# Sliding-window attention, start of the kernel: two of the first four row blocks of x turned by a transposing DMA, and one V chain moved ahead of the last Q and K group

## The chip, the cores and the metric

One core of one Trainium2 chip. The metric is device time of a whole execution in microseconds (us); medians of several runs are quoted. A ratio is the mean time of one kernel's fast runs over that of the other's fast runs of the same rounds, with a 95% interval, so it is not quite the ratio of two medians.

## The reference

Two independent problems A and B, outputs put side by side. Each is (x is 2048 x 1024, bf16):

```python
qkv = (x @ wqkv).reshape(B, S, 3, H, Dh).transpose(2, 0, 3, 1, 4)   # H = 32 heads of Dh = 32
scores = einsum("bhqd,bhkd->bhqk", q, k) * Dh ** -0.5
mask = (i - j >= 0) & (i - j < 256)                                  # sliding window
o = einsum("bhqk,bhkd->bhqd", softmax(where(mask, scores, -1e9)), v)
out = o.transpose(0, 2, 1, 3).reshape(B, S, D) @ wo
```

## The kernel before

TensorE does projections (Q, K, V, output), scores and attention sums. All of it is one static program: 180 steps. A step is the scores of four 128 x 128 blocks for four heads, one exponential over them on ScalarE, and then as many projection matmuls as a build-time clock finds room for ("filler"):

```python
def session(now):                      # the head of a step
    st = ps_st.tile([P, 4, SLOTS, P], F32, name="st")     # one buffer of four PSUM banks
    ...                                # scores on TensorE into st
    nc.scalar.activation(out=pt..., in_=st..., func=ACT.Exp, ...)

def new_pp():                          # a projection chain takes one of two PSUM banks
    clock.chain()
    return ps_proj.tile([P, 512], F32, name="pp")

def evacuate(out, in_, engines=("act", "dve")):           # ... and is copied out of it
    if clock.evacuate(engines) == "act":                  # which engine: by the build-time clock
        nc.scalar.copy(out=out, in_=in_)
    else:
        nc.vector.tensor_copy(out=out, in_=in_)

def emit(now, budget):                 # filler: matmuls of the chains, by deadline
    done = 0.0
    while (current or chains) and done < budget - ...:
        ...
```

The order in which chains come and the engine that copies each are fixed at build time. PSUM's eight banks: four for scores (`st`), two for attention sums (`acc`), two for projections (`pp`).

The start: x is loaded row-wise and turned on TensorE, block by block of 128 rows, for the first four blocks; all later rows come by transposing DMA.

```python
load_wqk(0, 0, nc.scalar)
for a in range(QB):                                        # QB = 4 row blocks
    nc.sync.dma_start(out=xrow[a], in_=problems[0][0][a * P:(a + 1) * P, :])
    if a == 1:
        load_wqk(0, 1, nc.sync)
load_wv(0, 0, CT, nc.sync)
new_x(0, 1)
load_x(0, 1)                                               # transposing DMA, rows 512 to 1023
...
warm = ps_proj.tile([P, 512], F32, name="pp")
keep_warm(6)                                               # dummy matmuls
...
flip(0)              # 8 transposes on TensorE, copied out half by ScalarE, half by VectorE
keep_warm(4)
flip(1)
keep_warm(3)
first(0, 0)          # Q of rows 0..255
flip(2)
flip(3)
first(1, 0)          # K of rows 0..255
first(0, 256)        # Q of rows 256..511, then its copy
first(1, 256)        # K of rows 256..511, then its copy
emit(0, chains[0].size)      # one V chain (rows 0..255); then the steps begin
```

Of the kernel before, what the change touches and what calls it, by code (L numbers as in the profile page):

```python
# [9 lines left out]
F32 = mybir.dt.float32  # L10
# [8 lines left out]
P = 128  # L19
# [7 lines left out]
QB = 4  # L27
SLOTS = 4
# [50 lines left out]
def _fast_path(ctx, tc, cfg, problems, outs, consts, certify):  # L79
    nc = tc.nc  # L80
# [8 lines left out]
    clock = _Clock()  # L89
# [27 lines left out]
    ps_st = ctx.enter_context(tc.tile_pool(name="ps_st", bufs=1, space=PSUM))  # L117
    ps_acc = ctx.enter_context(tc.tile_pool(name="ps_acc", bufs=2, space=PSUM))
    ps_proj = ctx.enter_context(tc.tile_pool(name="ps_proj", bufs=2, space=PSUM))
# [6 lines left out]
    blank = top[:].bitcast(BF16)  # L126

    def new_x(pi, k):
        xT[(pi, k)] = xpool.tile([P, CT, 512], BF16, name="xT")

    def load_x(pi, k, a=0, n=QB, c0=0, c1=CT):
        lo, hi = a * P, (a + n) * P
        nc.sync.dma_start_transpose(
            out=xT[(pi, k)][:, c0:c1, lo:hi],
            in_=problems[pi][0][k * 512 + lo:k * 512 + hi, c0 * P:c1 * P])

    def wsrc(pi):
        return problems[pi][1].rearrange("(ct p) (k n) -> p ct k n", p=P, k=3)
# [4 lines left out]
    def load_wqk(g, which, queue, lo=0, hi=CT):  # L143
        pi, t = divmod(g, T)
        queue.dma_start(out=wqk[g][:, lo:hi, which, :],
                        in_=wsrc(pi)[:, lo:hi, which, t * P:(t + 1) * P])

    def new_wv(m):
        wv[m] = wvp.tile([P, CT, VG * P], BF16, name="wv")

    def load_wv(m, lo, hi, queue):
        pi, mm = divmod(m, T // VG)
        w_ = VG * P
        queue.dma_start(out=wv[m][:, lo:hi, :],
                        in_=wsrc(pi)[:, lo:hi, 2, mm * w_:(mm + 1) * w_])
# [9 lines left out]
    def qk_tiles(g):  # L165
        if g not in qks:
            qks[g] = (qkp.tile([P, S], BF16, name="qT"), qkp.tile([P, S], BF16, name="kT"))
        return qks[g]

    def by_columns(out, lo, hi, lhsT, rhs, start, stop):  # L170
        if whole[0]:
            nc.tensor.matmul(out[:, lo:hi], lhsT=lhsT, rhs=rhs, start=start, stop=stop,  # L172
                             skip_group_check=True)
            return
        for c in range(0, P, 32):
            nc.tensor.matmul(out[c:c + 32, lo:hi], lhsT=lhsT[:, c:c + 32], rhs=rhs, start=start,  # L176
                             stop=stop, tile_position=(0, c), skip_group_check=True)
# [4 lines left out]
    def add_or(dst):  # L182
        def f():
            nc.vector.tensor_tensor(out=top[:], in0=top[:], in1=dst.bitcast(I32),
                                    op=ALU.bitwise_or)
        side.append((COST["or"], f, False))

    def evacuate(out, in_, engines=("act", "dve")):
        if clock.evacuate(engines) == "act":
# [4 lines that stand above are left out]
    def new_pp():  # L194
        clock.chain()
        return ps_proj.tile([P, 512], F32, name="pp")

    def qk_steps(g, which, k, lo=0, hi=512, st_=None, last=True):
        pi = g // T
        st_ = {} if st_ is None else st_  # L200
        steps = []
        for ct in range(CT):
            def f(ct=ct):
                if "pp" not in st_:
                    st_["pp"] = new_pp()
                by_columns(st_["pp"], lo, hi, wqk[g][:, ct, which, :], xT[(pi, k)][:, ct, lo:hi],
                           ct == 0, ct == CT - 1)
                clock.pe += NS_MM * (hi - lo) / 512.0
                if ct == CT - 1 and last:
                    dst = qk_tiles(g)[which][:, k * 512:(k + 1) * 512]  # L210
                    evacuate(dst, st_["pp"][:])
                    add_or(dst)
            steps.append((NS_MM * (hi - lo) / 512.0, f))
        return steps
# [138 lines left out]
    chains = []  # L353
# [39 lines left out]
    def start_chain(now):  # L393
        for n, c in enumerate(chains):
            if c.early <= now:
                current.extend(chains.pop(n).steps)
                return True
        return False

    def run_side():  # L400
        cost, f, last = side.pop(0)
        f()
        clock.dve = max(clock.dve, clock.pe) + cost
        if last:
            clock.norms.append(clock.dve)

    def emit(now, budget):
        done = 0.0
        while (current or chains) and done < budget - 0.5 * (current[0][0] if current else NS_MM):
            if not current and not start_chain(now):  # L410
                break
            ns, f = current.pop(0)
            f()
            done += ns
            if side and (clock.dve < clock.pe + 100.0 or len(side) > 8):
                run_side()
# [124 lines left out]
    rows = opool.tile([P, T, 512], BF16, name="oT")  # L541
    new_x(0, 0)
    new_wqk(0)
    new_wv(0)
    xrow = [rows[:, 2 * a:2 * a + 2, :].rearrange("p t n -> p (t n)") for a in range(QB)]
    load_wqk(0, 0, nc.scalar)
    for a in range(QB):
        nc.sync.dma_start(out=xrow[a], in_=problems[0][0][a * P:(a + 1) * P, :])
        if a == 1:
            load_wqk(0, 1, nc.sync)  # L550
    load_wv(0, 0, CT, nc.sync)
    new_x(0, 1)
    load_x(0, 1)
    new_wqk(1)
# [6 lines left out]
            new_wv(1)  # L561
            load_wv(1, 0, CT, nc.sync)

    warm = ps_proj.tile([P, 512], F32, name="pp")

    def keep_warm(n):
        for _ in range(n):
            nc.tensor.matmul(warm[:], lhsT=blank[:, 0:P], rhs=blank[:, 0:512], start=True, stop=True)  # L568

    keep_warm(6)  # L570
    flips = [ps_acc.tile([P, 512], F32, name="acc") for _ in range(2)]
    flips = [f[:] for f in flips]
    flips.append(ps_st.tile([P, 4, SLOTS, P], F32, name="st")[:, 0].rearrange("p a q -> p (a q)"))
    flips.append(None)
    held = [{}, {}]

    def flip(a):
        if a == 3:
            flips[a] = ps_acc.tile([P, 512], F32, name="acc")[:]
        f = flips[a].bitcast(BF16).rearrange("p (ct q) -> p ct q", q=P)  # L580
        for ct in range(CT):
            nc.tensor.transpose(out=f[:, ct, :], in_=xrow[a][:, ct * P:(ct + 1) * P],  # L582
                                identity=ident[:])
        dst = xT[(0, 0)][:, :, a * P:(a + 1) * P]
        half = CT // 2
        nc.scalar.copy(out=dst[:, :half, :], in_=f[:, :half, :])
        nc.vector.tensor_copy(out=dst[:, half:, :], in_=f[:, half:, :])

    def first(which, lo):
        for _, f in qk_steps(0, which, 0, lo, lo + 256, held[which], last=lo > 0):  # L590
            f()

    flip(0)
    keep_warm(4)
    flip(1)
    keep_warm(3)
    first(0, 0)
    flip(2)
    flip(3)
    first(1, 0)  # L600
    first(0, 256)
    first(1, 256)
    emit(0, chains[0].size)

    sealed = first_use(G - 1, NQ - 1, 0)
    for now in range(END):
# [3 lines left out]
        while due and due[0][0] <= now:  # L610
            _, pg, pk = due.pop(0)
# [14 lines left out]
    while due:  # L626
        _, pg, pk = due.pop(0)
# [132 lines left out]
def kernel(  # L760
# [48 lines left out]
    with tc.manual_schedule():  # L809
        with ExitStack() as fctx:  # L810
            _fast_path(fctx, tc, cfg, problems, outs, consts, [reduce_bits, decide])
# [40 lines left out]
```

## Time and profile before

| | before |
|---|---|
| median (6 runs) | 609.76 us |
| TensorE busy | 593.6 us, 98% of the span |
| first useful projection | 7.56 us |
| first scores | 13.83 us |
| waits of TensorE for ScalarE's copies | 4, together 1.6 us |

The prediction shows the lines of these. Two things help to read them. In a timeline line the columns are start, time, engine, line of the program, operation, operands, count, and in brackets the idle time ahead of it with what ended it. And the records have holes: of 330 matmuls of Q and K on 512 columns that this program has in its undivided form, the trace of before holds 291. The 3.5 us that TensorE seems to wait for "issue" are such holes (fewer matmul records than weight loads, 12786 against 12838 here), and busy times of two kernels are not comparable to a per cent. Starts are.

### The profile page before, as it was taken

What the parts mean: (1) busy time and instruction counts of PE and PEld (TensorE: products, weight loads), DVE (VectorE), ACT (ScalarE), POOL (GpSimd) and SP (SyncE); (2) the same over time, 40 slices, a digit from 0 to 9 for tenths busy, and PEclk for the clock granted to TensorE, in tenths of its full rate; (3) what the DMA queues carried; (4) which work ended last, traced back from release to release, by engine and by line L of the source; (5) the groups of instructions that cost most, each with busy time, mean ns of one, the idle gap of its engine ahead of it and who ended that gap; (6) DMA issues with size and microseconds to landing.
All of it is one profiled execution on the core that took longest, in us unless ns stands there. A gap on an engine that the chain in (4) does not pass through costs nothing.

```text
span 607.6 us, 28768 instructions
## 1 busy us (share of the span) xinstructions
PE 593.6 (98%) x12786; PEld 344.3 (57%) x12838; DVE 468.4 (77%) x1199; ACT 441.1 (73%) x376; POOL 326.3 (54%) x630
## 2 busy tenths in 40 slices
PE   8999999999999999999999999999999999999996
PEld 6555466656655756564556756655455665545443
DVE  1677889898898898897888887898888887897200
ACT  3778887788888887877778877777776777785332
POOL 0565666665666666556555565555555655554000
PEclk9999999999999999999999999999999999999999
DMA  9833110111015501442111100112021040113222
GB/s 234 182 92 89 37 38 3 38 38 39 3 38 90 114 14 30 82 101 77 38 37 38 38 4 8 33 37 81 2 68 34 4 106 21 55 58 120 72 79 64
DMA packets 86802, 35.47 MB, mean 58 GB/s; under 512 B 65552, under 2 KB 86160, under 8 KB 86672
## 3 DMA queue, kind: packets, MB, share of 16 engines
q1 hardware_dynamic: 85632, 33.31, 22.2%
q8 instruction: 102, 1.67, 1.2%
q10 hardware_dynamic: 1040, 0.26, 0.2%
q14 instruction: 28, 0.23, 0.1%
HBM read 17.83 MB, written 8.39 MB: 43 GB/s over the span
## 4 chain that ended last, share of the span: by engine, by line
PE 96%; ACT 2%; issue 1%; DMA 1%; ACTq 0%
PE pp L176 44%; PE pp L172 28%; PE acc L513 13%; PE st L451 10%; ACT pt L459 1%; DMA oT<-in_A_x_dram 1%; PE acc L582 0%; PE pp L568 0%; ACT kT L190 0%; ACT vt L190 0%; PE st L582 0%; ACT osb L190 0%; PE pp L805 0%; ACTq L190 0%
## 5 line engine op out<-in xcount | busy, mean ns | idle before, releaser
L459 ACT ACTIVATE pt<-st 128x2048 bf16<-128x2048 f32 x180 | 338.0, 1878 | 91.6 <-PE st L451 73.5
L471 POOL TENSOR_SCALAR_AFFINE_SELECT pt<-pt 128x512 bf16<-128x512 bf16 x224 | 154.5, 690 | 145.7 <-ACT pt L459 143.1
L467 POOL TENSOR_SCALAR_AFFINE_SELECT pt<-pt 128x512 bf16<-128x512 bf16 x256 | 179.2, 701 | 85.8 <-ACT pt L459 85.8
L524 DVE RECIPROCAL rinv<-acc 128x128 f32<-128x128 f32 x128 | 122.0, 953 | 57.0 <-PE acc L513 56.4
L176 PE MATMUL pp<-xT,wqk 128*32 128x512 bf16 x2712 | 163.1, 379 | 0.0
L481 DVE TENSOR_TENSOR both<-pt 128x512 bf16<-128x512 bf16 x224 | 137.1, 651 | 0.0
L176 PEld LDWEIGHTS <-wqk 128*32 128x32 bf16 x2712 | 69.3, 97 | 54.2 <-issue 0.4
L172 PE MATMUL pp<-xT,wqk 128*128 128x512 bf16 (+1 forms) x323 | 76.7, 369 | 4.1 <-issue 2.4
L176 PE MATMUL pp<-wv,xT 128*32 128x256 bf16 x2436 | 75.9, 273 | 0.0
L451 PE MATMUL st<-qT,kT 32*128 32x384 bf16 (+2 forms) x1488 | 71.5, 269 | 0.1
L176 PEld LDWEIGHTS <-xT 128*32 128x32 bf16 x2436 | 63.8, 97 | 6.2
L529 DVE STREAM_SHUFFLE wide<-rinv 128x128 f32<-128x128 f32 x256 | 64.6, 298 | 0.0
L513 PE MATMUL acc<-pt,vt 128*32 128x128 bf16 (+1 forms) x2160 | 63.3, 239 | 0.0
L172 PE MATMUL pp<-wo_sb,oT 128*128 128x512 bf16 (+1 forms) x269 | 59.3, 373 | 1.3 <-issue 0.9
L451 PEld LDWEIGHTS <-kT 32*128 32x128 bf16 x1488 | 22.2, 92 | 64.5 <-issue 63.3
L190 ACT CAST osb<-pp 128x512 bf16<-128x512 f32 (+1 forms) x52 | 30.0, 577 | 39.1 <-PE pp L172 24.4
L531 DVE TENSOR_TENSOR oT<-acc,wide 128x256 bf16<-128x256 f32 x128 | 54.3, 425 | 4.4
L176 PE MATMUL pp<-wo_sb,oT 128*32 128x512 bf16 x952 | 55.6, 379 | 0.0
L172 PEld LDWEIGHTS <-wqk 128*128 128x128 bf16 x362 | 33.4, 98 | 37.0 <-issue 6.8
L172 PE MATMUL pp<-wv,xT 128*128 128x256 bf16 x415 | 50.9, 273 | 1.4 <-ACT kT L190 0.6
L513 PEld LDWEIGHTS <-vt 128*32 128x32 bf16 x2160 | 35.9, 96 | 26.4 <-issue 24.1
L172 PEld LDWEIGHTS <-xT 128*128 128x128 bf16 x415 | 38.9, 98 | 12.0 <-issue 6.1
(46 smaller groups left out, 386.5 us busy)
## 6 DMA issues: line engine op xcount, KB each, us to landing
out_dram<-osb SPq DMA_DIRECT2D x63, 128.0 KB, 1.8
wqk<-in_B_wqkv_dram SPq DMA_DIRECT2D x32, 128.0 KB, 2.5
wqk<-in_A_wqkv_dram SPq DMA_DIRECT2D x24, 128.0 KB, 2.7
wo_sb<-in_A_wo_dram SPq DMA_DIRECT2D x16, 128.0 KB, 2.2
wv<-in_B_wqkv_dram SPq DMA_DIRECT2D x16, 128.0 KB, 2.8
wo_sb<-in_B_wo_dram SPq DMA_DIRECT2D x16, 128.0 KB, 2.4
oT<-in_A_x_dram SPq DMA_DIRECT2D x4, 256.0 KB, 5.4
wv<-in_A_wqkv_dram SPq DMA_DIRECT2D x2, 512.0 KB, 5.9
```

The source lines that it names most:

```text
L172: nc.tensor.matmul(out[:, lo:hi], lhsT=lhsT, rhs=rhs, start=start, stop=stop, skip_group_check=True)
L176: nc.tensor.matmul(out[c:c + 32, lo:hi], lhsT=lhsT[:, c:c + 32], rhs=rhs, start=start, stop=stop, tile_position=(0, c), skip_group_check=True)
L190: nc.scalar.copy(out=out, in_=in_)
L451: nc.tensor.matmul(st[:, r, a:b, :], lhsT=kT[32 * r:32 * r + 32, j * P:(j + 1) * P], rhs=qT[32 * r:32 * r + 32, q * P:(q + b - a) * P], st ...
L459: nc.scalar.activation(out=pt[:, :, :n, :].rearrange("p r a q -> p r (a q)"), in_=st[:, :, :n, :].rearrange("p r a q -> p r (a q)"), func= ...
L467: nc.gpsimd.affine_select(out=blk, in_=blk, pattern=[[0, 4], [1, P]], compare_op=ALU.is_ge, fill=0.0, base=0, channel_multiplier=-1)
L471: nc.gpsimd.affine_select(out=blk, in_=blk, pattern=[[0, 4], [-1, P]], compare_op=ALU.is_gt, fill=0.0, base=0, channel_multiplier=1)
L481: nc.vector.tensor_tensor(out=both[:, :, h, :], in0=pts[s0][:, :, a0, :], in1=pts[s1][:, :, a1, :], op=ALU.add)
L513: nc.tensor.matmul(acc[32 * r:32 * r + 32, o:o + w_], lhsT=lhsT, rhs=src[:, r, :, :], start=(x == 0), stop=(x == len(moves) - 1), tile_pos ...
L524: nc.vector.reciprocal(out=rinv[:], in_=acc[:, 2 * P:3 * P])
L529: nc.vector.stream_shuffle(out=wide[:, h * P:(h + 1) * P], in_=rinv[:], mask=[16 * h] * 32)
L531: nc.vector.tensor_tensor(out=oTs[(pi, k)][:, t, (p % 2) * 256:(p % 2 + 1) * 256], in0=acc[:, 0:256], in1=wide[:], op=ALU.mult)
```

## The change

The intent, as I read it: save 16 of the 32 transposes on TensorE by letting the DMA turn blocks 2 and 3, begin useful work earlier by treating blocks 0 and 1 one at a time, and fill the time until the DMA's rows arrive with the first V chain. The dummies and the first Q and K move into the score banks, which are not in use yet.

```diff
-    for a in range(QB):
+    for a in range(2):
         nc.sync.dma_start(out=xrow[a], in_=problems[0][0][a * P:(a + 1) * P, :])
-        if a == 1:
+        if a == 0:
             load_wqk(0, 1, nc.sync)
     load_wv(0, 0, CT, nc.sync)
+    load_x(0, 0, 2, 2)
     new_x(0, 1)
     load_x(0, 1)
 ... (cut)
-    warm = ps_proj.tile([P, 512], F32, name="pp")
+    spare = ps_st.tile([P, 4, SLOTS, P], F32, name="st")[:].rearrange("p r a q -> p r (a q)")
+    warm = spare[:, 1]
 ... (cut)
-    held = [{}, {}]
+    held = [{"pp": spare[:, 2]}, {"pp": spare[:, 3]}]
 ... (cut)
-    def first(which, lo):
-        for _, f in qk_steps(0, which, 0, lo, lo + 256, held[which], last=lo > 0):
-            f()
+    def first(lo, hi):
+        for which in range(2):
+            for _, f in qk_steps(0, which, 0, lo, hi, held[which], last=hi == 512):
+                f()

     flip(0)
-    keep_warm(4)
+    keep_warm(3)
+    first(0, P)
     flip(1)
     keep_warm(3)
-    first(0, 0)
-    flip(2)
-    flip(3)
-    first(1, 0)
-    first(0, 256)
-    first(1, 256)
+    first(P, 2 * P)
+    emit(0, chains[0].size)
+    first(2 * P, 4 * P)
+    clock.banks = [clock.pe, clock.pe]
     emit(0, chains[0].size)
```

So two V chains now stand ahead of the first scores, not one.

More of the change, by code (lines that the diff above doesn't have):

```diff
@@ L544, in _fast_path @@
     new_wv(0)
-    xrow = [rows[:, 2 * a:2 * a + 2, :].rearrange("p t n -> p (t n)") for a in range(QB)]
+    xrow = [rows[:, 2 * a:2 * a + 2, :].rearrange("p t n -> p (t n)") for a in range(2)]
     load_wqk(0, 0, nc.scalar)
-    for a in range(QB):
+    for a in range(2):
         nc.sync.dma_start(out=xrow[a], in_=problems[0][0][a * P:(a + 1) * P, :])
-        if a == 1:
+        if a == 0:
             load_wqk(0, 1, nc.sync)
     load_wv(0, 0, CT, nc.sync)
+    load_x(0, 0, 2, 2)
     new_x(0, 1)
@@ L562, in _fast_path @@
             load_wv(1, 0, CT, nc.sync)
-    warm = ps_proj.tile([P, 512], F32, name="pp")
+    spare = ps_st.tile([P, 4, SLOTS, P], F32, name="st")[:].rearrange("p r a q -> p r (a q)")
+    warm = spare[:, 1]
     def keep_warm(n):
         for _ in range(n):
-            nc.tensor.matmul(warm[:], lhsT=blank[:, 0:P], rhs=blank[:, 0:512], start=True, stop=True)
+            nc.tensor.matmul(warm, lhsT=blank[:, 0:P], rhs=blank[:, 0:512], start=True, stop=True)
     keep_warm(6)
-    flips = [ps_acc.tile([P, 512], F32, name="acc") for _ in range(2)]
-    flips = [f[:] for f in flips]
-    flips.append(ps_st.tile([P, 4, SLOTS, P], F32, name="st")[:, 0].rearrange("p a q -> p (a q)"))
-    flips.append(None)
-    held = [{}, {}]
+    flips = [ps_acc.tile([P, 512], F32, name="acc")[:] for _ in range(2)]
+    held = [{"pp": spare[:, 2]}, {"pp": spare[:, 3]}]
     def flip(a):
-        if a == 3:
-            flips[a] = ps_acc.tile([P, 512], F32, name="acc")[:]
         f = flips[a].bitcast(BF16).rearrange("p (ct q) -> p ct q", q=P)
```

## The prediction

> **What bounds the kernel now.** I read the page first (busy times, then the chain that ended last), then TensorE's waits, then the first 17 us of the chain, then single waits further on.
>
> From the page of the kernel before, busy time and chain:
>
> ```profile
> PE 593.6 (98%) x12786; PEld 344.3 (57%) x12838; DVE 468.4 (77%) x1199; ACT 441.1 (73%) x376; POOL 326.3 (54%) x630
> ...
> PE 96%; ACT 2%; issue 1%; DMA 1%; ACTq 0%
> ```
>
> TensorE is busy for 98% of the span and makes up 96% of the chain. So the end moves only by what is taken from or given to TensorE: fewer columns streamed, or fewer stalls. Everything else is hidden unless it stalls TensorE.
>
> The waits of TensorE over the whole span:
>
> ```profile
> PE pp L172 <- ACT vt L190: 1.0, 2, 0.5
> PE pp L172 <- ACT kT L190: 0.6, 2, 0.4
> PE pp L172 <- DVE oT L531: 0.3, 2, 0.2
> ```
>
> The columns are total us, times, longest. Only four waits for ScalarE come up in 600 us, 1.6 us together. I return to them, as a reordered program can have more.
>
> The head of the chain, 0 to 17 us (start, us, what):
>
> ```profile
> 0.80 3.50 DMA oT<-in_A_x_dram
> ...
> 4.34 1.04 PE acc L582 x8
> 5.38 0.90 PE pp L568 x4
> 6.28 0.60 PE acc L582 x8
> 6.89 0.65 PE pp L568 x3
> ...
> 7.56 1.06 PE pp L172 x8
> 8.62 0.45 PE st L582 x8
> 9.06 0.45 PE acc L582 x8
> 9.51 4.39 PE pp L172 x40
> 13.90 0.33 PE st L451 x8
> 14.23 2.07 PE pp L172 x17
> ```
>
> L582 is a transpose of a row block of x, L568 a dummy matmul that keeps the clock up, L172 a projection, L451 the first scores. The reader sees that useful projection starts only at 7.56 us, after two blocks are turned and copied, and that 0.90 us then go to turning two more blocks.
>
> The copies between a transpose and its first use, from the timeline (start, us, engine):
>
> ```profile
> 5.42 0.59 ACT L586 COPY xT<-acc 128x512 bf16<-128x512 bf16 x1 [2.84 <-PE acc L582]
> 6.04 0.42 DVE L587 COPY xT<-acc 128x512 bf16<-128x512 bf16 x1 [4.73 <-ACT xT L586]
> ...
> 6.92 0.59 ACT L586 COPY xT<-acc 128x512 bf16<-128x512 bf16 x1 [0.92 <-PE acc L582]
> ```
>
> The DVE half starts after the ACT half has ended (6.01), so a block is usable in halves. Block 1: transposes at 6.26, first matmul at 7.56, 1.30 us later.
>
> SyncE's issues from the timeline:
>
> ```profile
> 3.29 0.43 SPq L154 DMA_DIRECT2D wv<-in_A_wqkv_dram  x1
> 3.77 8.07 SPq L133 DMA_TRANSPOSE xT<-in_A_x_dram  x1
> ```
>
> The second 512 rows of x come by a transposing DMA, issued at 3.77 and landing 10.2 us later (the view of its tile), at about 14.0.
>
> **What the Trainium skill says.** (1) "TensorE: Matmul & The Clock Gate", section "Wait — 56ns, not 53.3ns?": warm matmuls follow each other at columns / 2.4 GHz plus about 2.5 ns, 55.6 ns for 128 columns. The trace agrees: 8 transposes in 0.45 us are 56 ns each, and 40 matmuls of 256 columns in 4.39 us are 110 ns each. So the row's "mean ns" (273 for 256 columns) is latency, not cost. (2) "PSUM — Partial Sum Buffer", section "PSUM bank collisions raise a hardware error": two engines must not touch one bank and quadrant at once, ScalarE against VectorE too. The trace shows the consequence above: VectorE's half of a copy out of the same bank waits for ScalarE's. The new code keeps that. (3) "Advanced Engine Details and Errata", section "X-Bar Transpose (TRN2)": transposing DMAs are as fast as plain ones. Here roughly: in windows of half a microsecond the stretch of only transposing traffic (10.5 to 13 us) moves 290 GB/s, the plain stretch before (6.3 to 9 us) 325.
>
> **The change part by part.** The order of the two programs, compared engine by engine, gives the counts.
>
> TensorE's work. Removed: 16 transposes and one dummy of 512 columns. Added: nothing in columns, but Q and K of the first 256 rows come in 32 matmuls of 128 columns in place of 16 of 256; that costs 32 x 56 - 16 x 110 = 30 ns. Moved: 16 V matmuls (4096 columns) from after the first scores to before them. All else has the same columns, and the count of switches between full, row-tiled and column-tiled matmuls is the same. Gross saving 0.90 + 0.22 us of TensorE's instructions.
>
> What it means for the clock time of the head, stepped with the durations above:
> - Block 0 turned at 4.34, ScalarE's half ready at 6.05, VectorE's at 6.50. Q, K on 128 columns: 4 matmuls at 6.05, the other 12 from 6.50 at 56 ns, to 7.17.
> - Block 1 turned at 7.17. Ready 1.30 us later, 8.47 (first half) and 8.92 (second). Here TensorE has only three dummies to do: a stall of about 0.85 us that the old order did not have after 7.56. Q, K of block 1 to 8.92 + 12 x 0.056 = 9.6.
> - V of blocks 0, 1: 16 x 0.110 = 1.76, to 11.35. Q, K of blocks 2, 3: 16 x 0.110 = 1.76, to 13.1. V of blocks 2, 3: to 14.9. First scores with their switch, 0.42: 15.3.
>
> The old kernel had done the same work (first scores and both V chains) at 15.92, where the timeline starts the next Q chain. So the head gains about 0.6 us, not the 1.1 of the removed instructions: turning block 1 now sits between useful pieces with its copy exposed. The scores start 1.1 us later than before (14.95 against 13.83), but 4096 columns (1.71 us) are already done; the following steps carry less filler until that is paid back, and TensorE stays the bound.
>
> The rest of the program. The scheduler's estimate is fixed at build time, so later steps get another mix of filler. A step (there are 180) is the scores of four blocks, one exponential on ScalarE, and projections as filler. Projections have two PSUM banks. If one step ends two chains' worth so that a third chain starts in it, the third needs the bank of the first; when ScalarE empties that bank it does so behind the step's exponential. One such case in the chain, with step 44's:
>
> ```profile
> 141.00 0.02 issue
> 141.03 1.88 ACT pt L459
> 142.90 0.49 ACT vt L190
> 143.39 0.04 issue
> 143.43 0.38 PE pp L172
> ```
>
> I went through the order of both programs for steps in which a third chain starts early while its bank is emptied by ScalarE in that step. For each, the start of the third chain after the first score matmul is 0.46 us (scores and switch), plus 0.62 us if attention sums are in the step, plus columns / 2400 per us. Before: steps 20, 44, 73, 79, at 2.59, 2.27, 2.38, 2.27 us. These are exactly the four waits in the trace (at 72, 141, 224 and 242 us); the view gives 0.5, 0.5 for the V ones at 2.27, and 0.4 and 0.2 for the others. So the wait is about 2.8 us minus that start. (Steps 129 to 159 have starts of 2.9 and later and show no wait, which fits.) After: steps 17, 23, 28, 41, 73, 79, at 2.38, 2.27, 2.59, 2.49, 2.38, 2.27: 0.4 + 0.5 + 0.2 + 0.3 + 0.4 + 0.5 = 2.3 us. That is 0.7 us more than the 1.6 of before. Cases emptied by VectorE (no exponential ahead) show no wait in the trace and number 11 before, 10 after.
>
> Sum: 609.6 - 0.6 + 0.7 = 609.7; nearly nothing. As the extra waits are certain in order but the head could gain a little more (a landing earlier with less traffic), I say 609.6 us.
>
> **Rivals.** (a) The full gain: the head saves 1.1 us or more and the extra waits vanish in other slack. For it: 98% busy, so each saved column counts. Against: four waits of this kind are on the chain already, one for one with the order. It would give 608.3. (b) The transposing DMA becomes the wait. Blocks 2 and 3 (0.5 MB) follow V's weights; by then 1.57 MB are queued ahead, against 1.09 MB moved by 6.3 us and 325 GB/s after, so weights end at about 7.9 and, at 290 GB/s, the blocks at 9.7, landing near 10.3. Needed at 11.35. The next 512 rows land near 14, as before, because the bytes ahead are the same; needed at 15.3 instead of 15.9. For this rival: margins of only 1 us, and issue of 512 rows took 5.6 to 8.1 us of SyncE, so a slow issue could add 1 to 2 us: 610.5 to 611.5. Against: the issue of 8.07 us was held up by the traffic ahead, as the later two took 6.00 and 5.61. (c) ScalarE becomes the bound in the early steps, since scores start later and less filler covers each exponential. A step needs 0.45 + 1.88 us for scores and exponential, TensorE's steps are about 2.9 us apart: slack of half a microsecond. If it did, all of the head's gain is lost, 610.3.
>
> **Range and chances.** Head 0.6 with an error of about 0.5, waits 0.7 with about 0.4, between runs the old kernel spreads by 1.2 us in all (609.18 to 610.35). So 608.5 to 610.7 eight times in ten. Two per cent are 12 us, more than the whole head could give or a late transfer take: faster 0.01, within 2% 0.98, slower 0.01.
>
> **What would show it.** Right: useful projection from about 6.05 us; scores at about 15; the chain after the head again TensorE; the waits of TensorE for ScalarE's copies up from four to six, about 2.3 us, near steps 17, 23, 28 and 41; TensorE's matmul count down by about 58 as some V columns run whole. Wrong: a wait of TensorE for a DMA of x in the head (rival b); waits for the exponential's PSUM in the first steps (c); a head that ends later than 15.9; or four or fewer ScalarE waits with a time below 608.5.

## The result, and the profile after

| | before | after |
|---|---|---|
| median (6 runs each) | 609.76 us (609.18 to 610.35) | 611.19 us (610.68 to 611.58) |
| ratio | | 1.0022 (1.0009 to 1.0035) |
| span of the profiled run | 607.6 us | 608.9 us |
| first useful projection | 7.56 us | 6.04 us |
| first scores | 13.83 us | 15.71 us |
| scores and both V chains done | 15.92 us | 16.04 us |

Within 2%, as said, but 1.4 us slower where I had said nearly nothing, and outside my range of 608.5 to 610.7.

The waits of TensorE over the span, after (total us, times, longest):

```profile
PE pp L172 <- ACT vt L190: 1.3, 3, 0.5
PE st L172 <- ACT qT L190: 0.7, 1, 0.7
PE pp L172 <- ACT kT L190: 0.6, 2, 0.4
PE pp L172 <- ACT qT L190: 0.4, 1, 0.4
```

The three rows with `pp` are the six stalls I had counted from the order: 1.3 + 0.6 + 0.4 = 2.3 us, as predicted. The row with `st` is new: Q and K of the start lie in `st`. It is in the head. The timeline there, after:

```profile
9.46 1.91 PE L172 MATMUL pp<-wv,xT 128*128 128x256 bf16 x16
...
11.29 1.03 PE L172 MATMUL st<-xT,wqk 128*128 128x256 bf16 x8
...
12.36 0.58 ACT L190 CAST qT<-st 128x512 bf16<-128x512 f32 x1 [0.37 <-PE st L172]
...
12.99 1.03 PE L172 MATMUL st<-xT,wqk 128*128 128x256 bf16 x8 [0.67 <-ACT qT L190]
...
15.71 0.40 PE L451 MATMUL st<-qT,kT 32*128 32x384 bf16 x8
```

The V chain and Q start within 0.2 us of my steps (9.6 and 11.35). Then K's eight matmuls stand still for 0.67 us until ScalarE has copied Q out, though they write another bank. The scores come at 15.71, where I had 14.95. The built program has this wait in it, at K's first matmul of the last group; the same matmul of the kernel before has none:

```
after   L172 Matmult st<-xT,wqk 128x256 [waits Activation_49]
before  L172 Matmult pp<-xT,wqk 128x256
```

The head is done (scores and both V chains) when the next Q chain starts. Before, in the line that the prediction speaks of, and after:

```profile
15.92 0.81 PE L172 MATMUL pp<-xT,wqk 128*128 128x512 bf16 x2
```

```profile
16.04 1.25 PE L172 MATMUL pp<-xT,wqk 128*128 128x512 bf16 x5
```

The stalls further on, seen in one step, number 17. In before (scores, next scores):

```profile
63.08 0.40 PE L451 MATMUL st<-qT,kT 32*128 32x128 bf16 x8
...
65.89 0.40 PE L451 MATMUL st<-qT,kT 32*128 32x384 bf16 x8
```

The same step after:

```profile
64.45 0.40 PE L451 MATMUL st<-qT,kT 32*128 32x128 bf16 x8
...
64.90 1.88 ACT L459 ACTIVATE pt<-st 128x2048 bf16<-128x2048 f32 x1 [0.59 <-PE st L451]
66.67 0.58 ACT L190 CAST qT<-pp 128x512 bf16<-128x512 f32 x1
...
67.30 0.59 PE L172 MATMUL pp<-xT,wqk 128*128 128x512 bf16 x2 [0.41 <-ACT qT L190]
67.83 0.40 PE L451 MATMUL st<-qT,kT 32*128 32x384 bf16 x8
```

Both have the same filler, 5632 columns. Before, the step takes 2.81 us from scores to scores; after, 3.38. The copy of a chain that ended early in the step waits behind the exponential, and a third chain needs its bank at 67. The wait row says 0.41, the step lost 0.57. Most of the difference is in the records: idle time is counted from the recorded end of the last matmul, and a record of 512 columns is 379 ns long on average (`--lines --by-form`), while such matmuls start 216 ns apart. So the row shows each stall about 0.16 us too short.

Done for all 180 steps (start of the scores in one kernel less that in the other, less the difference in filler so far at 0.216 us per 512 columns), the 1.3 us of the profiled runs divide like this:

| where | start of the third chain after the scores | after against before |
|---|---|---|
| head, to the first scores | | +0.15 |
| step 17 | 2.38 | +0.57 |
| step 20 (stalled in before only) | 2.59 | -0.34 |
| step 23 | 2.27 | +0.67 |
| step 28 | 2.59 | +0.35 |
| step 41 | 2.49 | +0.45 |
| step 44 (stalled in before only) | 2.27 | -0.67 |
| steps 49, 64 and 158 | | -0.09, +0.12, +0.19 |
| all other steps | | 0 within 0.03 each |

Steps 73 and 79 stall in both and cancel. The rows of the table add up to 1.40 us; the small differences of all other steps take 0.08 back. Every stall costs 2.94 us less the third chain's start, to 0.01 us; I had used 2.8 from the wait rows.

### The profile page after: what moved, and what is told of

It is laid out like the page before. It is cut to its first block, busy times and chain, and to the rows that moved or that the text cites. A ratio compares the mean times of both kernels' runs of the same rounds, so it can differ in the third digit from the quotient of the medians.

```text
span 608.9 us, 28698 instructions
## 1 busy us (share of the span) xinstructions
PE 599.1 (98%) x12780; PEld 344.0 (56%) x12780; DVE 467.5 (77%) x1196; ACT 440.5 (72%) x375; POOL 324.2 (53%) x630
## 4 chain that ended last, share of the span: by engine, by line
PE 76%; ACT 1%; issue 0%; ACTq 0%
PE pp L176 35%; PE pp L172 23%; PE acc L513 11%; PE st L451 8%; ACT pt L459 1%; ACT vt L190 0%; ACT kT L190 0%; ACT osb L190 0%; PE pp L802 0%; ACTq L190 0%
## 5 line engine op out<-in xcount | busy, mean ns | idle before, releaser
L172 PE MATMUL pp<-xT,wqk 128*128 128x512 bf16 x327 | 78.5, 380 | 0.7 <-ACT qT L190 0.4
L176 PE MATMUL pp<-wv,xT 128*32 128x256 bf16 x2348 | 73.4, 273 | 0.0
L176 PEld LDWEIGHTS <-xT 128*32 128x32 bf16 x2348 | 61.4, 97 | 5.5
L172 PE MATMUL pp<-wo_sb,oT 128*128 128x512 bf16 (+1 forms) x282 | 61.2, 373 | 0.0
L172 PE MATMUL pp<-wv,xT 128*128 128x256 bf16 x437 | 53.8, 273 | 1.6 <-ACT vt L190 1.0
L172 PEld LDWEIGHTS <-xT 128*128 128x128 bf16 x437 | 41.3, 98 | 13.1 <-issue 6.1
```

The lines of the kernel that those rows point to most:

```text
L172: nc.tensor.matmul(out[:, lo:hi], lhsT=lhsT, rhs=rhs, start=start, stop=stop, skip_group_check=True)
L176: nc.tensor.matmul(out[c:c + 32, lo:hi], lhsT=lhsT[:, c:c + 32], rhs=rhs, start=start, stop=stop, tile_position=(0, c), skip_group_check=True)
```

## The experiments

My theory after the result: the head loses its gain to K waiting for Q's copy, which is an order of the program and not of the hardware; the later steps lose 1.0 us because the V chain that moved ahead of the scores shifts the filler against the exponentials. Rivals: the transposing DMA is late or costs more than it saves; the stalls come from something else in the head.

Twelve kernels ran, all with a correct result. "Before" was timed again in each call (medians 609.49 to 609.71).

| label | edit | median us | ratio to before (95%) |
|---|---|---|---|
| e1_late_copy | changed, Q copied behind K | 611.62 | 1.0028 (1.0014 to 1.0042) |
| e2_dve_four | changed, four copies on VectorE | 609.52 | 0.9999 (0.9985 to 1.0012) |
| e4_one_chain | changed, one V chain first | 611.01 | 1.0021 (1.0007 to 1.0035) |
| e5_before_two | before, two V chains first | 610.54 | 1.0013 (0.9999 to 1.0026) |
| e6_dma_only | before, blocks 2, 3 by DMA | 610.91 | 1.0022 (1.0005 to 1.0038) |
| e3_before_dve | before, four copies on VectorE | 608.84 | 0.9987 (0.9974 to 1.0000) |
| c1_all | e1 and six copies on VectorE | 610.33 | 1.0010 (0.9997 to 1.0023) |
| e7_one_group | e1, rows 0 to 255 in one group | 611.91 | 1.0026 (1.0012 to 1.0040) |
| c2_best | e7 and five copies on VectorE | 609.16 | 0.9989 (0.9976 to 1.0003) |
| e8_more_dummies | e1, dummies cut in four | 611.89 | 1.0042 (1.0027 to 1.0057) |
| c3_before_three | before, three copies on VectorE | 609.02 | 0.9989 (0.9976 to 1.0002) |
| c4_all_dummies | e8 and five copies on VectorE | 610.19 | 1.0005 (0.9992 to 1.0018) |

### The V chain alone: e5_before_two

```diff
     emit(0, chains[0].size)
+    emit(0, chains[0].size)
```

> The kernel before with one added line: both V chains of the first 512 rows ahead of the first scores; no other part of the change. Its order has the early third chains at 17, 23, 28, 41, 73, 79, as the changed kernel. My theory: the head neither gains nor loses work (scores later by 1.7 us, with 4096 columns more done), and the later steps cost 2.04 - 1.01 = 1.0 us more than before: ratio 1.0017, +0.9 to +1.3 us. Rival (the loss of the changed kernel lies in its transposing DMA or smaller matmuls): within 0.3 us of the kernel before.

Measured: 610.54 us, 1.05 us above before, as written; the interval of the ratio just reaches 1 (0.9999), so the proof lies in the steps. TensorE's waits in this kernel, of which the third row was not there in before and the first was 1.0 in two:

```profile
PE pp L172 <- ACT vt L190: 1.3, 3, 0.5
PE pp L172 <- ACT kT L190: 0.6, 2, 0.4
PE pp L172 <- ACT qT L190: 0.4, 1, 0.4
```

Step by step against before: +0.57, -0.35, +0.67, +0.34, +0.45, -0.66 at steps 17, 20, 23, 28, 41, 44. One line, no transposing DMA for blocks 2 and 3, no other order of Q and K, and the later loss is there to 0.02 us a step.

### The change without the second V chain: e4_one_chain

```diff
     first(2 * P, 4 * P)
     clock.banks = [clock.pe, clock.pe]
-    emit(0, chains[0].size)
```

> The changed kernel with only one V chain ahead of the first scores, as before; the second follows them. The order of the program then has the early third chains at steps 20, 44, 73 and 79, exactly as the kernel before. My theory (the second V chain ahead of the scores is what shifts the filler and causes the stalls at 17, 23, 28, 41): no step after the head loses or gains against the kernel before, the later excess of 1.0 us is gone. But the first scores now stand right behind K's copy with nothing between, so the head ends about 0.8 us later than that of the kernel before: time 0.7 to 1.1 us above before (ratio 1.0012 to 1.0018), all of it lost before step 1. Rival (the stalls come from other DMA timing or PSUM placement in the head): waits stay at 17, 23, 28 and 41 and the time is 1.8 us or more above before.

Measured: no step after the head differs from before by more than 0.1 us; the head is 0.84 us later. Two rows of waits are its own:

```profile
PE st L451 <- ACT kT L190: 0.7, 1, 0.7
PE st L172 <- ACT qT L190: 0.7, 1, 0.7
```

So the scores wait for K's copy, as the V chain no longer lies between. The sum at the last scores is 0.92 us; the time is 1.5 us above by medians, 1.3 by spans, somewhat more than my 0.7 to 1.1. TensorE's last matmuls end 0.9 us later than in before, so 0.3 us of the span came behind them, in the last stores. Together e4 and e5 show the choice the change made: without the second V chain the copy is exposed for 0.7 us, with it the filler shifts for 1.0 us.

### The four copies: e2_dve_four

```diff
+    HANDED = (17, 23, 28, 41)
+    step = [-1, 0]               # step number, copies so far in its filler
     def evacuate(out, in_, engines=("act", "dve")):
-        if clock.evacuate(engines) == "act":
+        step[1] += 1
+        best = clock.evacuate(engines)
+        if step[1] == 1 and step[0] in HANDED:
+            best = "dve"
+        if best == "act":
```

> The changed kernel with four single PSUM copies (the first of steps 17, 23, 28 and 41) done by VectorE instead of ScalarE; the scheduler's clock is left as it was, so every other instruction keeps its place. My theory: these four cost 0.57 + 0.67 + 0.35 + 0.45 = 2.0 us, because each stands behind an exponential of 1.88 us. Then the four steps lose their excess and the time falls by about 2.0 us, to 0.6 us below the kernel before (ratio 0.999). Rival (VectorE, with its queue of normalisation, is no sooner free than ScalarE; or the stall has another cause, such as a late V or K load): less than 0.7 us comes back, and new waits of TensorE for VectorE's copies show in these steps.

Measured: 609.52 us. The changed kernel's 611.19 is from another call; each against the before of its own call, e2 is 1.4 us faster, not the 2.0 I had written, and level with before instead of 0.6 us below it. Step 17 in this kernel's timeline:

```profile
66.26 0.68 DVE L200 CAST qT<-pp 128x512 bf16<-128x512 f32 x1
...
67.51 0.40 PE L460 MATMUL st<-qT,kT 32*128 32x384 bf16 x8
```

Its scores started at 64.67, so the step takes 2.84 us again. Against the changed kernel, steps 17, 23, 28 and 41 give back 0.54, 0.16, 0.19 and 0.46, together 1.35 of their 2.04. In step 23 VectorE was not free in time: TensorE waits 0.4 us for its copy. So the place of the copy behind the exponential is the cause: at step 17, where VectorE was free, all but 0.03 us of the loss went. An engine with work of its own is a partial cure.

### The same on the kernel before: e3_before_dve and c3_before_three

The edit of e2 on the kernel before, with steps 20, 44, 73, 79, and then without 79.

> The kernel before with its four stalling copies (first of steps 20, 44, 73, 79) done by VectorE, the scheduler's clock untouched. My theory: of their cost, 0.34 + 0.67 + 0.57 + 0.67 = 2.25 us by the rule of 2.94 us minus the third chain's start, what VectorE's own queue leaves; in the run of this kind on the changed kernel 0.5 us stayed where the third chain starts at 2.27 and 0.0 to 0.2 at the others. So 1.0 to 1.3 us less than before (ratio 0.998). Rival (copies on VectorE only move the stall): no change within 0.3 us.

> The kernel before with only the copies of steps 20, 44 and 73 on VectorE; step 79 stays with ScalarE, since VectorE made it 0.2 us slower there. Expected from the step table of the run with four: 0.36 + 0.16 + 0.18 = 0.7 us below the kernel before, up to 0.9.

Measured: 608.84 and 609.02 us. Against before, e3 gains 0.36 at step 20, 0.16 at 44, 0.18 at 73 and loses 0.19 at 79: less than I had written, because at 44 and 79 the copy waits on VectorE for 0.7 us at the longest. c3 shows the three gains again, 0.70 together; it does not come out below e3, so the 0.19 at step 79 is not worth telling in whole times.

### Q's copy behind K: e1_late_copy

```diff
-            for _, f in qk_steps(0, which, 0, lo, hi, held[which], last=hi == 512):
+            for _, f in qk_steps(0, which, 0, lo, hi, held[which], last=False):
                 f()
+        for which in range(2 if hi == 512 else 0):
+            dst = qk_tiles(0)[which][:, 0:512]
+            evacuate(dst, held[which]["pp"])
+            add_or(dst)
```

> The changed kernel with one edit: Q's copy out of PSUM is issued after K's last matmuls instead of between them. My theory: K's matmul at 12.99 us waited 0.67 us only because the program orders it behind ScalarE's copy of Q, as Q and K lie in one tile. Then the wait row of TensorE for ScalarE's qT copy in the head (0.7 us) is gone, the first scores start near 15.0 instead of 15.7 us, and the time falls by 0.6 to 0.7 us against the changed kernel, to about 0.75 us above the kernel before (ratio about 1.0012). Rival (the transposed blocks of x arrive late, or are slow to read): TensorE stops at the same place for as long, and the time stays at 1.4 us above. The four stalls at steps 17, 23, 28 and 41 stay in both.

Measured: the wait for Q's copy is gone and the scores start at 14.97, as written. But the time does not fall (611.62). From its timeline, the scores and the next projection:

```profile
14.97 0.40 PE L451 MATMUL st<-qT,kT 32*128 32x384 bf16 x8
...
16.71 2.53 PE L172 MATMUL pp<-xT,wqk 128*128 128x512 bf16 x11 [1.34 <-DMA xT<-in_A_x_dram]
```

My theory of the wait held, and so, one step on, did the rival. The projection after the scores needs rows 512 to 1023, and these landed at 16.7 us, against 15.0 in the changed kernel. The completion records show why: 15 of the 16 DMA engines were done by 15.1, the last 1.6 us later. Head gain 0.59 us, wait 1.38 us in the first step.

### The DMA alone: e6_dma_only

The kernel before, with `range(2)` for the row-wise blocks, `load_x(0, 0, 2, 2)` behind the V weights, and the lines `flip(2)`, `flip(3)` taken out; nothing reordered.

> The kernel before with only the transposing DMA of the change: blocks 2 and 3 of x come by it behind the V weights, their 16 transposes on TensorE are gone, and the order of all else stays (V after all of Q and K, 256-column groups). My theory: the blocks land near 11.2 us, as in the changed kernel, while TensorE is through with the first half of Q and K at 9.3; it waits about 1.9 us for the DMA and saves 0.9 us of transposes, so the head is 1.0 us later and the time 0.8 to 1.3 us above before (ratio 1.0017), with the later steps unchanged (stalls at 20, 44, 73, 79 only). Rival (transposing by DMA frees TensorE at no cost, and only the order of V or the copies hurt): 0.9 us below before.

Measured: 610.91 us, 1.2 above before, with runs from 610.29 to 612.90. The rows land at 11.2 us and TensorE waits 1.95 us for them. The profiled run was one of the long ones (612.39). First a line of its timeline, then the stretch from 13 to 15 us of its table of stretches, whose last three columns are the granted clock (0.50), the DMA share and GB/s:

```profile
11.21 2.42 PE L172 MATMUL pp<-xT,wqk 128*128 128x256 bf16 x16 [1.95 <-DMA xT<-in_A_x_dram]
```

```profile
13.00:15.00 2.00, 2.00 (x11) 1.45 (x10) 0.75 (x2) 0.59 (x1) 0.00 (x0) 0.50 1.03 232
```

The clock fell to half at 12.46 us, 1.25 us after TensorE had gone on, and stayed there for 3.41 us (0.50 from 12.46 to 15.87), so the head came out 2.6 us late in that run. In the 3.41 us up to the fall TensorE had been busy for 1.46. The other long run, 612.90, has no profile; its mean granted clock, 0.996, is that of the profiled run, where the four others have 0.998 to 0.999, so the same cause is likely but not shown. These four, 610.29 to 610.97, are still 0.6 to 1.3 us above before, within the range I had written but for the lowest. The DMA for itself is a loss here unless other work fills the time to 11.2, which is what the moved V chain is for.

### All together, and the lagging engine: c1_all, e7_one_group, c2_best, e8_more_dummies, c4_all_dummies

c1 is e1 with six copies on VectorE (steps 17, 23, 28, 41, 73, 79).

> The changed kernel with Q's copy behind K's matmuls, as in the first run of this kind, and the copies of steps 17, 23, 28, 41, 73 and 79 on VectorE. My theory: first scores at 15.0 us. If the second 512 rows of x land at 15.0, as in four of the five traces, the head gains 0.6 us on the kernel before and the time is about 1.6 us below it. If one of the 16 DMA engines lags by 1.6 us again, as in the trace with the late copy, TensorE waits 1.3 us after the first scores and the gain is 0.3 us. So this run also tells whether that lag belongs to the earlier scores or was chance. Rival (late landing has nothing to do with it): no DMA wait and about 607.9 us.

Scores at 14.84, and the same lag of one engine: 1.25 us of waiting for x. The time, 610.33 us, is 0.6 above before, where I had written 0.3 below for this case: VectorE's copies leave 0.51 and 0.16 us at steps 23 and 28, and step 158 costs 0.48, which I cannot explain. So the lag came in both kernels with the earlier scores. In both traces one 16 KB packet of the kind "instruction" starts 0.7 us before the 15 engines are done. The Trainium skill, "Runtime: NRT & Kernel Launch", section "Instruction fetch mechanics", says that a sequencer refills its instruction memory in 16 KiB blocks of 256 instructions by DMA, mostly hidden. The size of the packet agrees; whose instructions it holds no run here shows. Two kernels move it.

```diff
 # e7_one_group, on top of e1
     keep_warm(3)
-    first(0, P)
     flip(1)
     keep_warm(3)
-    first(P, 2 * P)
+    first(0, 2 * P)
```

> The changed kernel with the late copy of Q and with Q, K of the first 256 rows in one group of 16 matmuls behind both turned blocks, instead of two groups of 16 on 128 columns. Two things are told apart. First, what the early 128-column groups are worth: my theory is nothing, since the V chain then ends near 11.2 us either way and the transposed blocks land at 11.2; scores stay near 15.0. Second, the lag of one DMA engine with the second 512 rows of x: in both traces with the lag, a 16 KB instruction packet lies on the DMA engines 0.3 to 0.5 us before the rows are in, and takes 1.15 us; the lagging engine is 1.6 us behind. With 32 fewer TensorE instructions ahead this packet should come 1 to 2 us later, after the rows; then they land at 15.0 in all engines, TensorE does not wait for them, and the time is 1.2 us below that of the late copy alone, 0.5 us above the kernel before (ratio 1.0008). If the lag has another cause that goes with early scores, the wait of 1.3 us stays and the time is as with the late copy (ratio 1.003). If the early groups were worth their intent, scores come 0.3 us or more later than 15.0.

> The same with the copies of steps 17, 23, 28, 41 and 73 on VectorE; step 79 stays on ScalarE, as VectorE made it 0.2 us worse. If the lag is gone: head 0.6 less than the kernel before, no stalls of its own at 20 and 44 (1.0 less), 0.5 and 0.2 left at 23 and 28, 0.2 less at 73: together 1.1 us below before, about 608.6. If the lag stays: 0.1 above before.

c2 is e7 with the copies of steps 17, 23, 28, 41 and 73 on VectorE; c4, below, is e8 with the same. In the traces of e7 and c2 the packet starts 1.8 us after the rows are in, and all 16 engines are done by 15.2: no lag, as written. But I was wrong about the early groups: without them TensorE has nothing to do until the second block is there.

```profile
7.20 1.03 PE L579 MATMUL acc<-ident,oT 128*128 128x128 bf16 x8 [0.72 <-DMA oT<-in_A_x_dram]
```

The transposes take 1.03 us here instead of 0.6: the clock was still at half (in the trace's clock records full speed begins at 10.4 us here and 10.8 in c2, at 5.9 in the changed kernel), and the scores came at 16.92 in this run. The packet is late here probably in part for the same reason. The runs of e7 fall apart: 610.57 and 610.77, and 611.91, 612.02, 612.35; I had written 610.1. Both profiled runs, of e7 and c2, are the longest of their five. So what the early groups are worth stays open: the idle time and the late clock show in the long runs, and the short runs, without a profile, are no slower than e1. c2, 609.16, is no faster than e3; I had written 608.6.

```diff
 # e8_more_dummies, on top of e1
-    keep_warm(6)                 # 6 dummies of 512 columns
+    keep_warm(24, P)             # 24 of 128 columns: the same TensorE time
```

> The changed kernel with the late copy of Q, and its first six dummy matmuls of 512 columns cut into 24 of 128: the same TensorE time, 36 instructions more ahead of everything. Only the place of the 16 KB instruction packet should move, 1 to 2 us earlier (from 14.4 us to about 12.5 to 13.5). If that packet just ahead of the end of the second 512 rows of x is what makes one DMA engine lag, the lag changes: either all engines land near 15.0 and TensorE's wait of 1.3 us is gone (time about 0.5 us above the kernel before), or the packet delays an engine wherever it falls in the transfer (lag stays, 2 us above before). If the packet does not move, or moves and the lag stays at 1.6 us to the tenth, the packet is not shown to be the cause.

> Late copy, 24 small dummies, and the copies of steps 17, 23, 28, 41 and 73 on VectorE. If the lag is gone by the dummies: 0.6 + 0.34 + 0.67 + 0.18 - 0.5 - 0.2 = 1.1 us below the kernel before. If it stays: 0.2 us above.

The packet moved to 11.8 us. Blocks 2 and 3 land at that moment, so it meets the start of the transfer of rows 512 to 1023. Now all 16 engines were late together: in e8's DMA view (`--dma --window 10:18`) they move 0 to 19 GB/s from 12.4 to 13.8 us, against 290 before the lag in e1, and the rows are in at 17.0.

```profile
17.08 1.24 PE L172 MATMUL pp<-xT,wqk 128*128 128x512 bf16 x5 [1.22 <-DMA xT<-in_A_x_dram]
```

c4 did the same: packet at 11.5, rows in at 17.3, wait 1.8 us, 610.19 (0.5 above before, where I had written 0.2 above for a lag that stays). My guess of 12.5 to 13.5 for the packet was off. e8's time is 2.2 us above before, near the 2 I had named for a lag that stays, but by luck: not one engine lagged but all. The traces fall into three groups: with the packet after the rows there is no lag (e7, c2), with it at the start of their transfer all engines finish about 2 us late (e8, c4), at the end one engine does (e1, c1). What stays open is the end: in the kernel before the packet starts 0.6 us ahead of the rows' landing, in the changed kernel 0.4, in e2 and e4 0.7, and in none of these do the rows lag; the packet itself took 1.4 to 1.5 us in the first two and 2.0 to 2.2 in e2 and e4, against 1.15 in e1 and c1. In these four one engine falls behind only in the next transfer, 0.8 to 1.8 us after the other 15 (e1 and c1 have such a straggler there too). That there it was the packet which waited for the rows, and in e1 and c1 the rows for the packet, fits, but no run here shows it.

No version beats both kernels clearly. e3 comes nearest: the upper end of its interval is 1.0000.

## Why the prediction was wrong

Point by point, by its own steps:

- "TensorE stays the bound": right. All steps but the listed ones have the same length in both kernels.
- Block 0, block 1 and the V chain: right to 0.2 us. The exposed copy of block 1 was there as told.
- "Q, K of blocks 2, 3: 16 x 0.110 = 1.76, to 13.1": this step failed. I let Q and K follow each other as before. Before, Q and K had PSUM tiles of their own, and K ran on during Q's copy (9.51 to 13.90 us without a gap in the chain). After, both are slices of one tile, and the program's order has a wait of K's first matmul for ScalarE. (That the shared tile put the wait there is read from the two programs; no run gives K a tile of its own.) I had counted instructions per engine but not read the waits of the new order. The wait row has 0.67 us; from Q's start to K's it is 1.70 us instead of 8 x 0.110 = 0.88, so the step cost 0.82. e1 took it away, and the scores came at 14.97, against 14.95 in the prediction. The head's term was +0.15 us by the one pair of profiles instead of -0.6.
- The extra stalls: right in number, place and wait rows (2.3 us), and e5 shows their cause. Mis-sized in time: the term was 0.7 us and measured 1.03. The idle time in the wait row is not all that a stall costs; the step loses about 0.15 us more, each time, since a matmul's record runs longer than its share of TensorE. The prediction had said of this length that it is "latency, not cost", and then took the idle time behind it for the whole cost.
- The transposing DMA (rival b): half right. It was no wait in the changed kernel, but the margins were overdrawn: blocks 2 and 3 landed at 11.2 instead of 10.3, just when TensorE needed them, and the next rows at 15.0 instead of 14, where the kernel before had them (13.95). Had K not waited, the rival would have come true in its place: e1 waited 1.34 us. I had called the issue time held up by traffic; the lag of one engine I had not thought of.
- Rival c: no ScalarE bound in the early steps; right.
- The matmul count: down by 58, right. The weight loads, one for each matmul and without holes in both traces, go from 12838 to 12780.

The sum: -0.6 + 0.7 was predicted. The two mis-sized terms give +0.15 + 1.03, with +0.2 at three further steps, of which the largest does not always repeat (step 158 shows it in e5 and c1 but not in e1 and e4), less 0.08 in all others, and so 1.3 us in the profiles, 1.4 in the medians.

The head's size has an error of its own. Three traces of programs with the same head as before have their first scores at 13.83, 13.61 and 14.54 us; in the last the dummies still ran at half clock at 5 us. Two with the head of the changed kernel have them at 15.71 and 15.93 (e2). The 0.15 is one pair; the six stalls repeat to 0.02 us in every kernel that has them.

## What to carry to other kernels

When buffers are re-used, read the waits of the new program and not only its counts: two halves of one tile can be tied together where two tiles were not. In a static schedule, moving one chain by one place moves all copies against all the long instructions behind which they queue; list the places where a bank is needed while its copy stands behind such an instruction, before and after, and price each from the start of one step to the next, not from the idle time. And when the head gets shorter, ask what lands next: here 0.6 us gained met a transfer with no margin.

## What the Trainium skill lacked or had wrong

- "TensorE: Matmul & The Clock Gate", the table of the two states, has the clock fall after an idle window of about 3.4 us. In one run here (e6) it fell though TensorE was idle for only 1.95 us: in the 3.41 us up to the fall, at 12.46, TensorE was busy for 1.46 us. It stayed at 0.50 for 3.41 us, and idle times of 1.34 us (e1) and 1.82 us (c4) had no fall behind them. The gap that the page gives for warm matmuls, columns / 2.4 GHz + 2.5 ns, agrees: 56 ns for 128 columns, 110 ns for 256.
- "Advanced Engine Details and Errata", section "X-Bar Transpose (TRN2)", expects 350 to 400 GB/s. A stretch of transposing traffic only held at 290 GB/s here (10.5 to 13 us of before).
- "Runtime: NRT & Kernel Launch", section "Instruction fetch mechanics", calls the cost of a refill mostly hidden. A 16 KB packet took 1.0 to 2.2 us on the DMA engines here, and in the two traces with it at the start of a 1 MB transposing transfer the rows landed about 2 us later (17.0 in e8, 17.3 in c4, against 15.0 in the changed kernel).
- None of the pages I read has the tie between two slices of one PSUM tile in different banks, 0.67 us of waiting here; it is the program's order, not the chip's, and e1 takes it away.
